# Token-mixing weights in pieces of at most 256 KB, and new instruction orders, in a two-layer attention and token-MLP kernel

## Chip, core and metric

The kernel runs on one core of a Trainium2 chip. The metric is the device time of one execution in microseconds, as the median of several runs. The core has five engines with queues of their own: TensorE (PE, with its weight loads shown as PEld), VectorE (DVE), ScalarE (ACT), GpSimd (POOL) and SyncE (SP). In this kernel SP does nothing but issue DMAs; "SPq" in a profile is SP's queue.

## What is computed

Two kinds of layer alternate, two times each, on one batch of 2048 tokens of width 512 in bf16. A is attention with 32 heads of 16 columns and a sliding window of 256 tokens; B is an MLP over the token axis (w1 is 2048 x 1792, w2 is 1792 x 2048).

```python
def _A_ref(x, wqkv, wo):
    H = 32; Dh = D // H; W = 256
    qkv = (x @ wqkv).reshape(B, S, 3, H, Dh).transpose(2, 0, 3, 1, 4)
    ...
    scores = einsum("bhqd,bhkd->bhqk", q, k) * (Dh ** -0.5)
    scores = where(mask, scores, -1e9)        # 0 <= i - j < W
    o = einsum("bhqk,bhkd->bhqd", softmax(scores), v)
    return o.transpose(0, 2, 1, 3).reshape(B, S, D) @ wo

def _B_ref(x, w1, b1, w2, b2):
    h = _layernorm(x)
    u = gelu(einsum("bsd,sf->bdf", h, w1) + b1)
    y = einsum("bdf,fs->bds", u, w2) + b2
    return y.transpose(0, 2, 1)

x = x + _A_ref(_layernorm(x), A_wqkv, A_wo)
x = x + _B_ref(_layernorm(x), B_w1, B_b1, B_w2, B_b2)
# and both once more
```

## The kernel before

Everything stays in SBUF: x as 16 tiles of 128 tokens, the normalised x (`xh_sb`), its transpose for the projections (`xhT`), masked copies of q and k, v, the probabilities (`p_sb`, seven slots) and the MLP's hidden `uT` in 14 tiles.

**Attention** runs over four groups Q of 512 tokens, four groups t of eight heads and nine steps m. A step is one `emit_scores` (matmuls on quarters of the array, L684), one exponential on ACT (`emit_exp`, L695), one or two multiplications by an edge mask (L712, on DVE or POOL), and one `emit_pv` (L733). That is 144 steps a layer. Two pairs of PSUM banks take the scores in turn, so step n + 2 waits for the exponential of step n. Between steps PE does other work: projections to q, k and v (L526), the output projection (L653), and products of the MLPs next to it. After every second head group four DMAs move denominators to `den_c` and numerators within `oU`.

**The MLP** needs all 16 token tiles for every hidden tile. `u_product` (L859) adds up one hidden tile (ft) from one quarter of the tokens, four matmuls at a time; `job_y` makes one output tile st from eight and then six hidden tiles (L932, the last tile of the kernel in two halves, L919). w1 is cut into seven blocks fb of 256 columns (two hidden tiles each), and each block into quarters q of the tokens. Blocks 0 to 2 lie in `w1buf`; they were loaded in halves of 512 KB (`w1_half_dma`). Blocks 3 to 6 borrow `xhT`, `k_sb` and `q_sb` once attention no longer needs them, in quarters of 256 KB (`w1_dma`); quarters 0 and 1 of block 3 share one tracked buffer in `xhT`, and quarters 2 and 3 the other. w2 is cut into eight blocks s2 of 256 output tokens, each loaded in two parts of 512 and 384 KB (`w2_dma`) into `w1buf` or `oU`; the later blocks follow when `job_y` has read the earlier ones.

**Order.** The program lists operations with what they read and write (`Plan.op`), and dependencies come from that. Which engine does an operation, and in what order, is written out in the tables `ORDER`: a string for each engine, in which two letters are the number of an operation in base 64 of `ALPHABET` ("AB" is operation 1, "BA" is 64). `BANKS` names the PSUM bank of each short-lived product. `emit` walks the tables and puts semaphore waits where a dependency crosses engines. An engine runs its list strictly in order; a DMA that has to wait on SP holds up all DMAs behind it. Every DMA also waits for the one that used its semaphore 16 DMAs ago.

At the start SP loads x tiles 0 and 1 (operations 0 and 1: AA, AB), tiles 2 and 3 (AC), four 256 KB parts of wqkv (AD to AG), the v part of wqkv, 512 KB into `w1buf` (AH), and x tiles 4 to 7 (AI); `turn_weights` (L437, L438) then rearranges that v part. The first normalisation (L460 to L476), a transpose on PE (L515) and its copy to `xhT` lead to half-projections (L562) and the first scores.

Of the kernel before, what the change touches and what calls it, by code (L numbers as in the profile page):

```python
# [33 lines left out]
O0OmOsO6NqPBOzO5PFM0PKPAPSQYPZPEPfPJPPPVPjPtNkPNPYPyPeP4PcPiPsQAQHPoPxP3P-QRO3QGQVQKQbP7QoQfQkRXQvQUQaQeQ1Q-Q5QjQuRDORRKQ0Q4ROQsRUQ+RHRcQERhRNRTRbRmRg
RlRzR0RRSuR3R4R5SvSrSsS3S0S4SxSGS1S2SDS6S5SRSJSySVS7SNSwStSoSlSzSpSmSqTHSnTDTFTBTZS9S8S-TaThTNTVTOTiTRTSTWTdTeTLTJT0UFT5UGT1T6UAUBUqUUUvUZUjUfUrUdUbUk
VQU8UVUhUoUwVAVEVSVIWjWkVMVWVbYeVpVkYfVhVuV1VaX5X6VyV6VjVoV+VtV0V5WGWTWoV9WNWFWVWDW4WfWaWKXYXGWRWwWrXHWZW1WeW9WqWvW0XCZoW8XBXNXUXdXrYzXiXnZeYCXwXcX1Xh
XmXvX0X-YXYMYHaNZ3YTYaX+aOYuYGYLYQY1a+Y6YZY-Yta-ZEZIYyY5Y+ZDZPalZZZHZOZSZhboZrZlZMbpZyZgZ5cLZ+ZkZqZxaCbHaKZ1aVaHZ9aiaBaJaSaeaYayadarahbEaqaaaxa6a5bDbS
cObNbldZbMbhcPbybRb2babVb6cjcDbkbtb1cIb5aucbcCcHcgdrcocNcfcsa1c0clc4eVdAcrczdEbudRc3c-dDdQdVdUdcb9ehdmdbduc7dzdfeFd5eAcvdteHdyd4d-eMgIeQeDeYeueeeLeneP
eXeberd2ezfLe7emfDejeqfIeye6fCfQe2fVfHfPfUfcfjfrfnfvgrfmfzfqfyf3gff-f2gFe+gLf+gEgQiLgYgKgPgcgVh8gkgogTgbgwgjgngvg0fYhBgzhFf6hQhkhbhAhfiohEhmhMhKhqhxhU
h0h1h4heh-hjhNhpiDhwh3iIiaiQh+iCiXiHiNiehOiiibisixiWiTidihi3iriwi2i-ili+jGjKjHjRjYkZjVjUjbjojfi6jkjajejwkAj2jjj6jskEjvj1kLjtkPj5j-kWjDkIkejEkjkOkVkdko  # L40
kiknk1k2kSkTk5k6k7lwl8l5lzl2l9l6lIltlulFl3lxlXlPl0lLlTlylvl1l4lqlrlsl7mHmJmBmPmjmDmQmFlnmTmkmblomXmfmgmUmcmYl+lpl-mLmNmzm9m+mvnDnEm5m6mwnHnIm0nNnbnjnf
# [5 lines left out]
NzMYMXMvL5MmL6MHNRM8MzMnNhL7NVNWNbMIMTN3NiNjMUMoOPOMO-N9OgN-MVOZOoPnOrOCOwOxNrM1O9QZOBPWPXPRM2PbPOPhPdP6PpPqQJO4QLQMQXP8P9QdQCQDQTRYQpQqQrQhRAQ3QyOSRB
QtP+RIRJRZRCRoRpRaRsRqRSR6R7RxQFRvSASCSHSISFSESSSKSWSXSTSOSLSPSMSQSUSYSZSbSfSgTbTPTjTTTXTfUHT7UKT2T+T3UCT-ULUDT4UEUOUMUaUTUgUeUcUsU9UlU+UmUiUnUWUxUtVC
VFUyVGUXWlUuUzUYVNU0VLVYVOU2VeVVYgYjVmVnU4ViV3VxVrX7V4WmVzWAWUWpWJV8WEW5WnWXWMW6W7X8XaWPWYYkX9WcWQXIW3XLXbZpXMYlXWXPY0XEXtXXXlXFZfXpXyYDYYX3YnYBYsYqXq
YpZ4YPYEYSYVYRY3YxaPY4Y8Y9bAZBZKZUbBanZTZNbqZuZtbCZncMZ7ZvbrZ8aAaFaIaUaXaTaZatacbJa0bGaba8aQdacQbncRbUb0aRbsbccSbWckbXcTawcGavcVcddscicqbYcucncma2cXc6  # L50
# [1016 lines left out]
```

## Time and profile before

| | us |
|---|---|
| three runs | 489.77, 489.77, 489.91 |
| median | 489.77 |
| profiled execution | 490.92 |
| its span | 489.2 |
| PE busy in the span | 480.0 (98%) |
| DVE / ACT / POOL busy | 335.3 / 319.7 / 199.6 |
| DMA moved | 43.59 MB, mean 89 GB/s |

The granted TensorE clock was 1.0. How to read it: the busy time of PE comes from pipelined matmuls whose ends are modelled, so its share is no measure of free room. An idle time stands with the engine that waited, and behind an arrow the instruction that ended the wait. A row of the table by stretches has the stretch, its length, the busy time of each engine with its number of instructions, the clock, the share of the DMA engines and the rate in GB/s. A row of the timeline has the start, the length, the engine and line, and what is written from what.

### The profile page before, as it was taken

The numbers are of one execution on the slowest core, as the hardware profiler recorded it, in microseconds if no ns is written. First come the engines' busy times: TensorE is split into PE (matmuls) and PEld (weight loads), VectorE is DVE, ScalarE is ACT, GpSimd is POOL, SyncE is SP. The second block draws the span as 40 slices with busy tenths as digits, with TensorE's granted clock in tenths as the row PEclk, the third lists the DMA queues.
The fourth block names the chain that finished last, engine by engine and source line by source line (L and its number), as shares of the span: only waits on it lengthen the run. The fifth ranks groups of instructions, "written<-read, shape, count | busy, mean of one in ns | idle before, by whom it ended". The sixth has DMA issues, their size and how long they took to land.

```text
span 489.2 us, 17263 instructions
## 1 busy us (share of the span) xinstructions
PE 480.0 (98%) x7706; PEld 255.4 (52%) x7706; DVE 335.3 (69%) x707; ACT 319.7 (65%) x391; POOL 199.6 (41%) x365
## 2 busy tenths in 40 slices
PE   7999998999999999999999999999999999999997
PEld 6544555555556444444445555556556544444444
DVE  7999998889988550246798777999977646122123
ACT  4999998999989313302767889999999940240000
POOL 5988884534726100022624544465644721000000
PEclk9999999999999999999999999999999999999999
DMA  6442024400228780350024300130222957030842
GB/s 194 92 119 56 27 60 100 70 5 27 27 58 223 215 228 1 107 147 5 1 44 132 89 27 3 37 62 6 68 70 77 261 148 204 0 98 10 228 150 86
DMA packets 83722, 43.59 MB, mean 89 GB/s; under 512 B 19008, under 2 KB 82624, under 8 KB 83648
## 3 DMA queue, kind: packets, MB, share of 16 engines
q1 hardware_dynamic: 79776, 42.48, 32.1%
q0 software_dynamic: 3872, 0.02, 1.2%
q8 instruction: 60, 0.98, 0.8%
q14 instruction: 14, 0.11, 0.1%
HBM read 32.51 MB, written 2.10 MB: 71 GB/s over the span
## 4 chain that ended last, share of the span: by engine, by line
PE 91%; ACT 5%; DMA 1%; DVE 1%; SPq 1%; issue 0%
PE ps L859 20%; PE ps L932 19%; PE ps L526 17%; PE ps L684 14%; PE ps L733 12%; PE ps L653 6%; ACT p_sb L695 4%; PE ps L777 1%; DMA x_sb<-in_A_x_dram 1%; PE ps L919 1%; SPq L352 1%; PE ps L446 0%; DVE o L358 0%; DVE q_sb L537 0%; ACT vT L360 0%
## 5 line engine op out<-in xcount | busy, mean ns | idle before, releaser
L695 ACT ACTIVATE p_sb<-ps 128x1024 bf16<-128x1024 f32 (+8 forms) x288 | 261.1, 974 | 23.5 <-PE ps L684 18.5
L712 POOL TENSOR_TENSOR p_sb<-p_sb,edge 128x256 bf16<-128x256 bf16 (+2 forms) x223 | 106.8, 494 | 102.7 <-ACT p_sb L695 88.0
L684 PE MATMUL ps<-q_sb,k_sb 64*64 64x288 bf16 (+8 forms) x2816 | 107.2, 250 | 1.4 <-ACT p_sb L695 1.1
L526 PE MATMUL ps<-xhT,wqkv 128*128 128x512 bf16 x376 | 95.6, 382 | 0.2 <-DVE q_sb L537 0.2
L733 PE MATMUL ps<-p_sb,v_all 64*64 64x288 bf16 (+8 forms) x2816 | 89.7, 246 | 1.6 <-DVE o L358 1.1
L684 PEld LDWEIGHTS ps<-q_sb,k_sb 64*64 64x64 bf16 x2816 | 53.6, 106 | 53.4 <-ACT p_sb L695 32.9
L733 PEld LDWEIGHTS ps<-p_sb,v_all 64*64 64x64 bf16 x2816 | 58.4, 107 | 14.8 <-issue 5.5
L932 PE MATMUL ps<-uT,w1buf 128*128 128x512 bf16 x280 | 64.3, 380 | 0.0
L936 DVE SCALAR_TENSOR_TENSOR x_sb<-ps,b2col,x_sb 128x512 bf16<-128x512 f32 x31 | 22.6, 745 | 51.0 <-PE ps L932 50.9
L712 DVE TENSOR_TENSOR p_sb<-p_sb,edge 128x256 bf16<-128x256 bf16 (+2 forms) x177 | 45.3, 275 | 14.1 <-ACT p_sb L695 12.7
L526 PEld LDWEIGHTS ps<-xhT,wqkv 128*128 128x128 bf16 x376 | 30.6, 98 | 39.7 <-issue 5.4
L482 POOL TENSOR_TENSOR rstd<-vare,mhalf 128x4 f32<-128x4 f32 x15 | 15.2, 1015 | 86.3 <-DVE vare L480 48.6
L859 PE MATMUL ps<-xh_sb,w1buf 128*128 128x512 bf16 x192 | 46.3, 381 | 0.0
L460 DVE BATCH_NORM_STATS2 stats<-x_sb 128x6 f32<-128x512 bf16 x64 | 42.9, 681 | 1.8 <-DMA x_sb<-in_A_x_dram 1.6
L932 PEld LDWEIGHTS ps<-uT,w1buf 128*128 128x128 bf16 x280 | 26.3, 98 | 32.3 <-issue 1.3
L537 DVE TENSOR_TENSOR k_sb<-ps,half 128x1024 bf16<-128x1024 f32 (+1 forms) x29 | 34.7, 1197 | 5.0 <-PE ps L526 4.9
L492 ACT ACTIVATE xh_sb<-x_sb,shift,rstd 128x512 bf16<-128x512 bf16 x8 | 6.4, 810 | 48.1 <-POOL shift L486 48.1
L537 DVE TENSOR_TENSOR q_sb<-ps,even 128x1024 bf16<-128x1024 f32 x29 | 35.3, 1217 | 1.9 <-PE ps L526 1.5
L932 PE MATMUL ps<-uT,oU 128*128 128x512 bf16 x154 | 35.5, 380 | 0.0
L653 PE MATMUL ps<-wo_sb,oT 128*128 128x512 bf16 x128 | 32.4, 381 | 0.0
L859 PE MATMUL ps<-xh_sb,k_sb 128*128 128x512 bf16 x128 | 30.8, 380 | 0.0
L586 POOL TENSOR_TENSOR v_all<-vB,v_all 128x512 bf16<-128x512 bf16 (+1 forms) x16 | 23.5, 1474 | 16.8 <-DVE vB L601 16.6
(89 smaller groups left out, 453.1 us busy)
## 6 DMA issues: line engine op xcount, KB each, us to landing
w1buf<-in_B_w_dram SPq DMA_DIRECT2D x20, 512.0 KB
oU<-o SPq DMA_DIRECT2D x16, 256.0 KB
k_sb<-in_B_w_dram SPq DMA_DIRECT2D x16, 256.0 KB
w1buf<-in_B_w_dram SPq DMA_DIRECT2D x10, 384.0 KB
oU<-in_B_w_dram SPq DMA_DIRECT2D x6, 512.0 KB
oU<-in_B_w_dram SPq DMA_DIRECT2D x6, 384.0 KB
q_sb<-in_B_w_dram SPq DMA_DIRECT2D x8, 256.0 KB
xhT<-in_B_w_dram SPq DMA_DIRECT2D x8, 256.0 KB
```

Source lines behind the costliest of these rows:

```text
L460: dve(lambda e: e.bn_stats(stats[:, t, :], x_sb[:, t, :]), 690, prio, reads=[R("x", t)], writes=[R("stats", t)])
L526: last = e.matmul(ps[:, b, :], lhsT=wqkv[:, c, c0:c0 + P], rhs=xhT[:, buf, c, :], start=(c == 0), stop=(c == 3))
L537: return e.tensor_tensor(dst, src.unsqueeze(2).to_broadcast([P, n, 2, w]), mask[:].unsqueeze(1).unsqueeze(3).to_broadcast([P, n, 2, w]), o ...
L586: return e.tensor_tensor(d, src.unsqueeze(2).to_broadcast([P, k, 2, DH]), v_all[:, 0:32].rearrange("p (h d) -> p h d", h=2).unsqueeze(1).t ...
L653: last = e.matmul(ps[:, b, :], lhsT=oT[:, buf, t, i * P:(i + 1) * P], rhs=wo_sb[:, t, :], start=(t == 0), stop=(t == 3))
L684: last = e.matmul(ps[64 * c:64 * c + 64, 2 * half + r, 32 * i0:32 * i1], lhsT=k_sb[rows, ring, t, kb % 16, :], rhs=q_sb[rows, t, c, 32 * i ...
L695: latest[0] = plan.op({ACT: (170 + int(2 * (512 - c0) * 0.84), lambda e: e.activation(p_sb[:, slot, :, c0:512], ps[:, 2 * half:2 * half + ...
L712: return e.tensor_tensor(v, v, g, op=ALU.mult)
L733: last = e.matmul(ps[64 * r:64 * r + 64, B_O + (c ^ r), 32 * i0:32 * i1], lhsT=v_all[rows, col:col + 64], rhs=p_sb[rows, slot, r, 32 * i0: ...
L859: r = e.matmul(ps[:, b, :], lhsT=blk[:, n, (ft % 2) * P:(ft % 2 + 1) * P], rhs=xh_sb[:, 4 * g + n, :], start=(first and g == quarters[0] a ...
L932: r = e.matmul(ps[:, b, :], lhsT=blk[:, fc, (st % 2) * P:(st % 2 + 1) * P], rhs=uT[:, fc, :], start=(fc == 0), stop=(fc == NFT - 1))
L936: dve(lambda e: e.scalar_tensor_tensor(x_sb[:, st, :], ps[:, b, :], b2col[:, st:st + 1], x_sb[:, st, :], op0=ALU.add, op1=ALU.add), 750, prio,
```

## The change

All loads of w1 and w2 are at most 256 KB. `w1_half_dma` issues two quarters, and what used to be tracked as a half of a `w1buf` block is tracked as two quarters, so that a `u_product` waits for its own quarter alone. `w2_dma` issues four parts of 4, 4, 4 and 2 hidden tiles instead of two of 8 and 6, each with its own part of the buffer; `job_y` still multiplies in steps of 8 and 6. That makes 42 more DMAs (2553 operations become 2595). All five order tables and the table of banks are new: 82 of the mask multiplications go from POOL to DVE and 86 the other way, 26 other operations from DVE to ACT and 27 back, and each engine's order differs. The operations on PE are the same.

```diff
     "tensor": """
-AuAvAwAxAyBLAzBJA0BPBNBTBRBVBXDTCuB1CeA1BpA2CjCoA3CcCyC3D1C9CnDEBtDKCxDOC2C8DXDDBxDJDeDmDNDkB5DxDVDsDbDBGsD4D9DiDrEFECDwEKFZD3D8EaEBEPGQEpEJEOETEjEeE3
+AuAvAwAxAyBJAzBLA0BPBNBTBRBVBXDTA1CeB1BpCoA2CjCuC3CyCcD1A3DEC9CnBtCxDKC2C8DODkDXDeDDDJDNDVDbDmBxDsDxDBB5D9DiD4DrGuDwECEKEFFaEPD3EaD8GSEjEBEJEOETEqEeEv
 ...
     "scalar": """
-AjAlBMBQBUBWBYDUB2CfBqCkCpAoCzC4C+DFBuDLDPDYByDfDnDlDtDyDCD5D+EDELEGEbEQEqEkEUE4EvEfE9FCEzFKFPFWFdFTFyF5F+GDGJGNGUGeGmGqIDGwG3G+HDHHHPHWHfHjHsHzH7IAIJ
+AlAjAiBMBQBUBSBYAmAnCfB2CpCkCvC4CzD2C+DFBuDLDPDYDfDnByDdDyDtB6D+D5GvEDELEGEQEbEkErEwEfE5E+E0FDFLFQFXFeFUFzF6F-GEGLGPGWGgGoGsGyG5HAHFHJHRHZHiHmHvH2H+ID
 ...
     "sync": """
-AAABACADAGAEAIAHCiAFCwDjCsDIDSCtC7DWDqHKGgGhEXEWG6EYEZGaGbGZGcKlEnK+IYIaKkIbHRLOIZKTKfKdKeKgMZMcMbMaOcObOaOdP2TxQPQNQQPwPrQOOWIvQiQzQnRfTnRyR8R+R9OlRk
-R-SkLkSiQ9GGRGTzTySjTlTmToTwT9UIT8UJWCVfVgWSXJYhXRXQXKXSXTYiZ2ZdZcaGZVZXZWZYbebdbfbgdpeUdqeEdkdjdidlfffidxfhfghTgDhZhYhXhamrhijPjNiqjQi1mnjOmsivj+j0e5
+ABAAACAIAEADAGAHAFCiCwCsDjCtDSDIC7G8GiEWHMEZDWEXEYGjEnEoDqGdGcGbGeIcIbLTIdHTHUIeKqLDKpKjKiKkKlMfMhMgMiKXKYOhOiOgOjQTQUQtQoQVQWP2P8RDPxR4OcRlQ5SDSCSERM
+SFSqRqSpIyIzSoT6T7T8T9OrGHGILpLqT+T-UAUBTrTsTtTuTvTwTxTyUYUZUaUbUKULUMUNWkVyVxWUY1Y2Y3Y4XbXcXdXeXmXkXnXlaMZzZyacZrZtZsZubzb2b0b1eAebd-erd5d6d4d7f4f3fQ
 ...
-        load(w_nat, w_src[:, :, 2 * D:3 * D], 1 << 19, -100, writes=[R("w1", 2, 0)])
+        load(w_nat, w_src[:, :, 2 * D:3 * D], 1 << 19, -100, writes=[R("w1", 2, 0), R("w1", 2, 1)])
 ...
-                return w1buf[:, fb, 4 * q:4 * q + 4, :], [R("w1", fb, q // 2)]
+                return w1buf[:, fb, 4 * q:4 * q + 4, :], [R("w1", fb, q)]
 ...
         def w1_half_dma(fb, h, prio):
-            load(w1buf[:, fb, 8 * h:8 * h + 8, :], w1v[:, 8 * h:8 * h + 8, fb * 256:(fb + 1) * 256], 1 << 19, prio, after=latest,
-                 writes=[R("w1", fb, h)])
+            for q in (2 * h, 2 * h + 1):
+                load(w1buf[:, fb, 4 * q:4 * q + 4, :], w1v[:, 4 * q:4 * q + 4, fb * 256:(fb + 1) * 256], 1 << 18, prio, after=latest,
+                     writes=[R("w1", fb, q)])
 ...
-                return flat[:, 0:NFT * 256].rearrange("p (f s) -> p f s", f=NFT), [[R("w1", k, h)] for h in range(2)]
+                return flat[:, 0:NFT * 256].rearrange("p (f s) -> p f s", f=NFT), [[R("w1", k, h)] for h in range(4)]
 ...
-                    [[r for t in (2 * h, 2 * h + 1) for r in held_o(k - 2, t)] for h in range(2)])
+                    [held_o(k - 2, t) for t in range(4)])
 ...
-            for h, (lo, hi) in enumerate(W2_PARTS):
+            for h, (lo, hi) in enumerate(((0, 4), (4, 8), (8, 12), (12, NFT))):
                 load(dst[:, lo:hi, :], w2v[:, lo:hi, s2 * 256:(s2 + 1) * 256], (hi - lo) << 16, prio, reads=after, writes=held[h])
 ...
-                pe(f, 217 * (hi - lo), prio, reads=held[part] + [R("uT", fc) for fc in range(lo, hi)], writes=[BK(b)])
+                pe(f, 217 * (hi - lo), prio, reads=held[2 * part] + held[2 * part + 1] + [R("uT", fc) for fc in range(lo, hi)], writes=[BK(b)])
```

More of the change, by code (lines that the diff above doesn't have):

```diff
@@ L34 @@
[L34 to L41, printed above, removed]
@@ L47 @@
[L47 to L50, printed above, removed]
@@ new lines @@
+NYLsLWL0LaNRL7LlMDLiLrMILzL6MQMCL3MVMHMPMjNHMrMnMUMcMvN2MzMmM3L+M-MqMyNENmNKM2M+NTNWNdNDNjMYNtNJNQNaNzNgN7NiN-OUNsOMNyN6OQPEOZN+OLOkOPOWOdOoOtOvOnOsOz
+PsO6OyPANwO5PHO-PLQeM6PYPGPKPQPPPbPlPVPfPTPzPePkPpPoNqP+P4PiPyQGP3P9PuQNQFQMQXO9QQQbQhRdQuQlQqOXQaQ1QgQkQpQ7RFQ-Q0RJQBRQQ6Q+RERUQKRaRNRiRXRnRTRZRhRmRs
+RrR5R6QyS0R9R+R-S3S6S7S9SxS1TASMS+S4SJTBS2SXSPSySTSbS8S5SrSsS-TCStTLTTTNTUSzTHTjTJTXTDTfTbSuTcTYTkTgTnToSvSwTFTPTRUCUDUHUQURUIUVUWVBU8U9U1UxUvU2UrUtVC
+U6UzUmVOViVaVkVzVSUnW1VoVtW2VWV7V2YyWEYzWAWHVsV1VeYNWMV6WQV-WGWLWYW6YOWPWnWfWlWVWXWxWcWsXKXsXYWjXCW9Z+XZXHWrWwXPW8ZJXUXoXBZ0XxXGXOXTXhX2YWX-X7YEXwX1Yr
@@ new lines @@
+YJYTX6ajYbYDYIYgaNYnYSYaYfYuakZEYkZLbUZQYtZDZIZVZPZaa7ZeZUZZZlbVZdZvZkZoZ3b+Z7aBZib-aIaPZ2chZ6aUaAaHaYbdaLagaradaTa4aXafaoa0aubIazbBa3baawbAbQbHbPbZbo
+ckbjb7biclbnb3bwcMdvcIb6cDcZc5cQbrcLcecPbEcxcYcdc2eBc+cjdCbLc1dKc7dOesdWdBdJdacEdndNdVdrcTdydZdmd8e4eEdqeKdFeQdxd1eXeceeeDeJePejdReneWeaevfFe1eie+gheN
+emfCfKeueyfjfTe9fbe6fgfBfJfSfofNftfafffnfsf0f7f-gDhEgHgLg4f+gPgCgKgXfWgegOgWgkilgpgdgxiWg1gjgogug9gshBhJfwhNg0g8hAhah+hehIhMhZhqhdhmhuh1gSjCh5iAhkiEiO
+iLh4h9iSiPiZiDiKidhniiiRiYiqi0ixicihini4i1i8jGhojLiwi3i7jRitjFjZjKjQjYjhi-jrjgjkjvjyj1kzjuj5j0j+kakCkKj4j9kQjUkUkJkPkTkekZkiklkGkskpkwkHktk4k9jdkolCkv
@@ new lines @@
+k3k8lBlQlPjelTlUlVmQmWmHmNmKmRmIlimSmJlfmXmTlpllmLmUlxmVltmMmOmPmEmFmGmYmfmdmtmum1mxmhmjmpmymbm5mqm6m2m9mBmCm+mDmZmnmlnVnpnhndntnqnunenWninRnSn5n1oJn6
+oFoBn2oVoGoNoCoKoWoRoZoSoOoaogod""",
+    "vector": """
+AcAdAeAfAgAWAUAVAaAYA7A5A8AQA6BBA-A9BDBAA+BFBEBKBIBHBdBOARBfAXBWBZBbAhDUBgAbAZBqBrBcCgBaBeBhBsBjCrChCdFjBoC0BnC1FlAsBmDGFhBvDlBwFnFiDcDgFoBzDoDCFmFkDu
+DzFpFrB0JJB7EAB8D0JNFbEHGTEUEVEsENJKEIEgEhE1E-ExGlFAF4JPFVFMFYFNJLFGFHF1HpFIGBHqGQGGHrHcJMIGGaGZHOIHGzIIG+G0JOJQG1HGJTIUHLHWHXHeIVHjHnHfI5JRH3H-HzHyIA
@@ new lines @@
+INIXIOKsIoIaIZItIpIlKaI6JuJFJbH5JBJVJcIqI8JHJ6JlJkH6JiJ7K2KEKAKFJvLwH7J8JwKGKVLhKIKgLVLxKLMMKNKMLILFK7K8LRLZLfNZLcLbNSLjLkMFL9MKL4L5MTLyNIMeMdMsN3MXN4
+MxL-MAMNM1NnM5NGN5NoNXNpMZNcNbNhMOMtNlOVMBMuOCODPFOTObOeOfOuOFOmOqOxMaPtNxPCO2O1QfO3M7POPaPcPWPXPnPdPUP1PjP7M8PvPwM9O+QRQIQJQdReQPQvQSRfOYQ4RGQ9QnRHQw
+QCRPROQDQxRYQERgRIRwRuRpQzRyR8SBSASGQLSISNSOR3SKSLSYSQSZSUSRScSdSeSVSSSaSWShSfSkSmTVTdTlThTpTZUEUJUOUSUFUXUcUTUGUPUUUdUgUeUjUlUyUwUsUuU+U3U4VDU0U-VjU5
+VAV0VcUoVQUpVRUqVTVEW3VFVvVUVwVIVGVXVMVNVVVnVYY0VZV+VfVKVqY5V4V5WJVgW7WOYPWmWpYQYRWhVhWiWdXMWeXNW4WbW5XuY6XaW0XfZKXRZ1XXXvXiXgXqY7YAXrYBY9ZBYsYLX+YHYV
@@ new lines @@
+YdYeYiaOYmYpZGYlalZHYxZOYYZSZTZca8YZama9bWa-a+ZpZjcAZ5aEbXaFciaSaaabaGaDaWaeaiaqapavbfanbKa6bDaxaybSbqbccBcCbYcmbybxbhdwcOc6cnbtbGbucobFcpeCc0c4bMcrc8
+c9cwcvcFetcUdtducVcGd+e5d3d2dGeddSeTfGdHeUeheZfHdIeqeOe0ezfkdTe8e7fdflfVfPdUfOf2bNgEfrf1cHhFhGg5gFgGg6bOfXdggNfYimdefZiXg7hHgvgwhRgtgzdldjfxhLg-hQhch-
+hThYfyhXhvhsjDhhhliHiCh3iQfziNiJikgUifizipi2ioigi+hpiviujTjOjAjbjmjBjtjljcjxk0j7kDkMkbkNjVkEkck1kdkWkFk2gVjWjXlGkXkIlIkrkylElFk-lSlNkulWjflclMleljlklh
+lglqlrlmlnlslylzlulvlol0lwl3l1l7l6l5mvmzmrm3m7m-nXnjnrnTnvnfn7n3oHoXoDoLoToPobohoe""",
+    "scalar": """
@@ new lines @@
+AlAjAiBMBQBUBSBYAmAnCfB2CpCkCvC4CzD2C+DFBuDLDPDYDfDnByDdDyDtB6D+D5GvEDELEGEQEbEkErEwEfE5E+E0FDFLFQFXFeFUFzF6F-GEGLGPGWGgGoGsGyG5HAHFHJHRHZHiHmHvH2H+ID
+IMIRIgIkA4IsIwI2I-JEJaJfJnJrJzJ3J-KDKQKUKdKnKvKhKzK5LALHLMLQLYLeLnNPLtL1L8MEMJMRMWMkMoMwM0M4NANFNLNUNeNkNuN0N8OAONOROaOlOpOwO0O7PBPIPMPZPRPmPgP0PqNrP5
+P-QHQOQYQcQiQmQrQ2Q8RARKRRRVRbRjRoRtR7R2SHR1SlTMTKTITETOTWTeTqTiTaTmTGSnTQTSU7VPVbVlVpVuV8V3WFWIVLWBWNWZWRWoWgWWXLWyWtXtXDW+Z-XIXQXVXpXyX3XjX8YFYXYKYC
+YUYcYhYoYvZFZMZRZWZbZfZmZwZqZ4Z8aCaJaQaVaZbeasaha5a1bJbCbbbRbpbgbkb8b4cNcJcacRbscfcyc3c-dDdLdPdXdbdodsdzd9eFeLeReYefekeoewe2e-gifDfLfUfcfhfpfuf8gAgIgM
@@ new lines @@
+gQgYgfglgqgyg2g+hChKhOhbhfhrhwh2gTh6T5iBiFiMiTiIiaieijiriyi5i9jHjMjSjajijsjwj2jzj6j-kLkRkVkfkmkjkkkqkxk5k+lDlRlXl9lKldmemgmimwmkm4msm0mcm8manAmomm""",
+    "gpsimd": """
+AJAMAKANASALATAOAPBCBGCEB+CJCDCHCKAoCLArCCCBCMCNApCOB3CqClAqBiB4BkCmBlC5AtC-DHDADMC6CPAkDZDaCQDhDQDRDpCRFqFsD-DvFtFvCSEED6D7FwCTERCUEMElEcESEmFuEdEtCV
+CWE6EyE7FEE2FRFZFfFSF0FgGACXCYF7GFF8GXB9GMGhGRCZHsGtGpHBG6B-HCHKG2HSHaIJCIHwJSJUJWIEISIWJYIhCAJXIxCGJACFI3JgJoJsJ0J4I7KRKeKoKHKJKwKWK6K0KKLBLNLJLSK9L2
+LoLuMGMSMpCaMlNBNCNfNVNMNNN1NvOBN9OOOSOEOGOIOKOHPDO8PJOJPNO4PSPhMbPrP6CbQAQZQjQsQ3RBRCRLRWRSRcRkRvRxRzR0SgSiSjUfUhTzUiUkVmT1T4T3VdV9VHVJVrWCWDWKT2WSWa
@@ L66 @@
+WzWTWqWuXEW-XAXJXFWvT0XWXSX4XzY8X0YGY+ZCX5ZAX9Y-YMYjYwZNYqZXZYZgZnZhZxZ9aKaRata2bTblbmb9b5cKcbcccgcSczbvcqcsdAcudEdQdMdYdcctdpddd0cWeGcXeMeSegexeVepel
+fIfEfAe3fMfifefqgBfvf9gJfmgZgggagmgRgrdfgng3dhdihShDdkhPhghUhWhVh7iUiGibiVi6isjIjNjjj3kAkSlHkglJknlLk6l2l4l8""",
     "sync": """
[L67 to L68 removed]
@@ L70 @@
+nUnsoEoMnooQoUocoIoiof""",
 }
 BANKS = (
-    "76766776777676767667766666677676777767776666667677677767666776666776676767677677667767766777666767676776776666677766676776776676677676676676"
-    "766677666777777667666776777676766767776666776776766776677766")
+    "76676666677777767667766677767676676777766766677677667767776667766766677776777667676766677676677766767676766667676766676776776676676677676676"
+    "766667776776766777666667676776766767776677777666676767677677")
 class Res:
@@ L438, in turn_weights @@
                      ACT: (360, lambda e: e.activation(d, o, ACTF.Copy))},
-                    reads=[R("w1", 2, 0)], writes=[R("wqkv", 2, t, r)], prio=-96)
+                    reads=[R("w1", 2, 0), R("w1", 2, 1)], writes=[R("wqkv", 2, t, r)], prio=-96)
         for t in range(4):
@@ L921, in f @@
                         return r
-                    pe(f, 1530, prio, reads=held[0] + held[1] + [R("uT", fc) for fc in range(NFT)], writes=[BK(bank)])
+                    pe(f, 1530, prio, reads=sum(held, []) + [R("uT", fc) for fc in range(NFT)], writes=[BK(bank)])
                     dve(lambda e, half=half, bank=bank: e.scalar_tensor_tensor(
```

23 lines of the change are left out of this document (3 added, 20 removed).

## The prediction

> **What bounds the kernel now.** I read the page's busy shares first, then cut the span at the first and last exponential of each attention (an ACT answer of the timeline gives 14.62, 159.38, 235.30 and 393.76 us) and asked for a table of these five stretches, then for ACT's own waits inside them.
>
> ```profile
> PE 480.0 (98%) x7706; PEld 255.4 (52%) x7706; DVE 335.3 (69%) x707; ACT 319.7 (65%) x391; POOL 199.6 (41%) x365
> ```
>
> ```profile
> core 0: us, PE busy (x) PEld busy (x) DVE busy (x) ACT busy (x) POOL busy (x), PEclk, DMA share, GB/s
> 0.00:14.62 14.62, 11.25 (x127) 9.15 (x128) 11.29 (x41) 7.90 (x14) 9.32 (x28) 1.00 0.54 163
> 14.62:159.38 144.76, 141.91 (x3272) 80.45 (x3269) 132.02 (x272) 138.52 (x165) 94.43 (x177) 1.00 0.34 74
> 159.38:235.30 75.92, 75.92 (x460) 35.02 (x459) 33.66 (x66) 20.36 (x31) 9.76 (x12) 1.00 0.40 112
> 235.30:393.76 158.46, 158.14 (x3332) 87.37 (x3330) 130.49 (x282) 140.33 (x167) 82.12 (x144) 1.00 0.27 71
> 393.76:489.20 95.44, 92.77 (x526) 43.41 (x523) 27.83 (x48) 12.62 (x20) 3.97 (x7) 1.00 0.40 113
> ```
>
> The rows say: the two MLP stretches (75.9 and 95.4 us) are PE and nothing else. The first attention is ACT's: 138.5 of 144.8 us busy, 6.2 us idle. The second attention is shared: ACT is idle for 18.1 us of 158.5, DVE for 28.0, and PE shows 158.1 us busy, which the page warns is not PE at its peak. Who keeps ACT waiting stands in its waits, of the first attention and of the second:
>
> ```profile
> ACT p_sb L695 <- PE ps L684: 4.9, 12, 1.4
> ```
> ```profile
> ACT p_sb L695 <- PE ps L684: 13.6, 27, 1.1
> ```
>
> So in the second attention ACT waits 13.6 us for scores that PE delivers late, because y and projection work is threaded between them; there the order on PE matters. No line of PE's own waits names a DMA. A weight that comes late would be a new wait.
>
> **How I read the diff.** Two letters of a table are an operation's number, so both sets of tables can be written out and compared entry by entry; a split load takes two numbers. SP's list grows from 194 to 236 entries (10 halves of w1 and 32 halves of w2 become pairs). In all 42 places the two pieces follow each other directly, so no other transfer is slipped between them. What is new comes from the order of whole loads, from readers that wait for one quarter, and from the moved instructions.
>
> **Start.** Three lines hold the first exponential back:
>
> ```profile
> 10.25 0.69 DVE L460 BATCH_NORM_STATS2 stats<-x_sb 128x6 f32<-128x512 bf16 x1 [0.91 <-DMA x_sb<-in_A_x_dram]
> 11.32 0.77 PEld L562 LDWEIGHTS ps<-xhT,wqkv 128*128 128x128 bf16 x8 [0.93 <-DVE xhT L358]
> 14.62 1.92 ACT L695 ACTIVATE p_sb<-ps 128x1024 bf16<-128x1024 f32 x2
> ```
>
> DVE stands 0.91 us for x tiles 4 to 7, the copy of xhT queues behind it, and PE's second half-projection waits for that copy. In the new table this x load is SP's fourth entry, not its seventh (AI follows AC), ahead of three 256 KB weights, so it no longer holds DVE. Against that, DVE now builds five edge tiles before its first statistics, about 0.3 us late, and ACT runs two weight turns (0.42 us each) before its first exponential. Followed through with the rows' durations: first statistics 3.1 (was 2.87), half-projections at 9.9 and 10.9 (were 9.64 and 11.32), three masks of 0.84 us on ACT end at 13.0, the turns at 13.85. That is 0.8 us sooner than 14.62; without the turns' cost elsewhere it could be 1.5, with a late weight 0. Taken: **-0.8** (-1.5 to 0).
>
> **First attention.** ACT's extras between its 144 exponentials change by: one v copy less (0.61), one k mask less (two of 0.64), two o copies less (1.20), one turn (0.42) and one reciprocal copy (0.31) less; two q masks more (2.54) and one u copy more (0.62). Sum **-0.6**, on the engine that sets the end. DVE gains some 1.2 us of work here beside 12.7 us idle; I price it at nothing, and at +1.2 if that cover is gone. Masks of p change hands between DVE and POOL (82 one way, 86 the other), which leaves the sum of each nearly alone.
>
> **First MLP: the rush of loads.** After the last score SP issues the rest of w1. Before:
>
> ```profile
> 167.19 0.77 SPq L352 DMA_DIRECT2D k_sb<-in_B_w_dram  x1
> 168.00 0.62 SPq L352 DMA_DIRECT2D xhT<-in_B_w_dram  x1
> 168.66 0.66 SPq L352 DMA_DIRECT2D w1buf<-in_B_w_dram  x1
> 173.40 0.37 SPq L352 DMA_DIRECT2D xhT<-in_B_w_dram  x1
> ```
> ```profile
> 158.50:178.00 19.50, 19.50 (x174) 9.08 (x173) 11.83 (x24) 4.20 (x6) 1.62 (x3) 1.00 0.80 223
> ```
> ```profile
> 178.60 1.89 PE L859 MATMUL ps<-xh_sb,xhT 128*128 128x512 bf16 x8
> ```
>
> SP stood 4.0 us before 173.40 for the landing of the piece issued at 168.00, which shares xhT's buffer; so a 256 KB piece took 5.4 us in this crowd. The new order keeps those two far apart, and SP's stand goes. But it puts w1's fb 3, quarter 1 after three den_c loads and twelve more, among them four w2 pieces (896 KB) whose reader comes some 59 us later. PE first needs that quarter one u step of 0.86 us sooner than at 178.60, about 177.7. Twelve issues at 0.62 us after 163.73 give an issue at 171.2. Bytes from 158.5 on: 1.05 MB of w1 released by the last scores, then 3.28 MB up to and with this quarter, 4.33 MB. At the best rate that the slices show (261 GB/s at a share of 0.95, so 275 at most) it lands near 176; at the 223 GB/s of the row above, near 179.5. Price 0 to +3.4 (the start moves the need 0.8 sooner); I take **+0.5**, nearer the fast end, since the old rush had SP's 4.0 us stand in it, which lowers its rate. The Trainium skill ("DMA: Bandwidth & Descriptors", section "Anatomy of one DMA") gives a transfer about 2.0 us and its bytes over 436 GB/s: by that an estimate for 256 KB is 2.6 us where the row has 5.4, the rush would take 10 us, and this term would be 0; the trace speaks against the rate under load.
>
> **Second attention.** Six y matmuls (1.3 us at the 0.216 us that 120 take in 25.90 us of the chain) and two projections (1.7 us) move from the first MLP behind the second attention's first score. The MLP loses 3.0 us; the attention gains 3.0 if PE is its limit, nothing if PE only waits there. They land in its first 20 us, where ACT is busy for 60 to 80% of a slice and PE is the limit, so most comes back. In the rest the filler is spread more evenly: counted in full-size matmuls between scores, 18 steps at a time, it ran 38, 42, 36, 32, 40 after the first 36 steps, and now 40, 42, 36, 36, 36. ACT gets 3.0 us of extras more, beside 18.1 us idle. Bounds -3.0 to +1.5; taken **-1.0**, from the even spread and a third of the moved work.
>
> **Second MLP and end.** 16 w2 loads become 32 pieces; the tightest, for y tile 9, is released 7.8 us of PE work before its use (7.4 before). The issues cost SP 42 x 0.37 to 0.77 us = 16 to 32 us over the span, on a queue that mostly waits. The output stores come in another order, the last half tile last as before. Priced at **0** (0 to +1.5).
>
> **Sum.** -0.8 - 0.6 + 0.5 - 1.0 + 0 = -1.9 us. The profiled execution took 490.92 us with a span of 489.2 (1.7 us lies around it) and is 1.15 over the median of 489.77, so the median becomes **487.9**, a profiled span 487.3. A measurement of this kernel can tell about 0.2%, 1.0 us, from no change.
>
> **Rivals.** (a) *A late weight on PE.* Place: the first u step on fb 3 in the first MLP, with a twin in the second, where fb 5's quarter 2 is read 6.5 us of PE work after the last PV and issued 2.6 us after it. It decides if the first lands after 177 us. At 223 GB/s PE stands 2.5 to 3.4 us; a 5.4 us flight makes the twin 1.5 us late. With the other gains: 489.77 - 2.4 + 3.0 + 1.5 = 491.9, slower. For: SP's list, with w2 ahead of w1. Against: no PE wait on a DMA in the old trace with a similar crowd. 0.29. (b) *Nothing.* The pairs stay together, so splitting does nothing but double issues; the start's gain is eaten by the first attention, where 6.2 us of ACT's idle time moves about. 489.5; 0.15. (c) *Larger gain.* Half of the 13.6 us that ACT waits for scores in the second attention goes, 5 us after DVE's part: 485.0; 0.11.
>
> **How the numbers follow.** Forecast 0.45 at 487.9 (own range 486.3 to 489.0, its top just over the 1.0 us line), (c) 0.11, (b) 0.15, (a) 0.29. Faster takes the forecast and (c), less a little: 0.55; within 0.2% takes (b): 0.15; slower 0.30. The range reaches from (c) to (a): 485.0 to 492.0; a lateness of both stages beyond 3.4 and 1.5 us, or a gain over 5, is left out.
>
> **What would show it.** First exponential near 13.9 us. First attention 143.5 to 145 us long, with ACT's idle time near 6. No gap of SP like that before 173.40. PE's waits: a line "<- DMA xhT<-in_B_w_dram" would mean (a). The second attention with ACT waiting less than 13.6 us for L684; more than that would make the forecast wrong there, as would a first exponential after 14.6.

## The result: 0.17% slower

The changed kernel took 490.66 us (median of 13 runs, 489.1 to 491.43) against 489.67 us for the kernel before (13 runs, 488.82 to 490.15): ratio 1.0017, 95% interval 1.0009 to 1.0025. The forecast of 487.9 us was 2.8 us too low, and the sign was wrong.

The profiled execution after took 490.62 us, close to its median; its span is 488.9 us. That of before, 490.92 us, was 1.25 us over its median, so the two profiles laid side by side (488.9 against 489.2) hide the loss. The five stretches of the changed kernel, cut as before at the first and the last exponential of each attention:

```profile
core 0: us, PE busy (x) PEld busy (x) DVE busy (x) ACT busy (x) POOL busy (x), PEclk, DMA share, GB/s
0.00:13.29 13.29, 11.64 (x132) 10.38 (x132) 10.41 (x36) 8.52 (x15) 7.79 (x24) 1.00 0.65 199
13.29:158.15 144.86, 142.29 (x3271) 80.00 (x3264) 133.54 (x278) 138.39 (x162) 98.56 (x181) 1.00 0.28 61
158.15:230.71 72.56, 71.81 (x440) 33.10 (x439) 31.31 (x62) 15.99 (x25) 7.25 (x11) 1.00 0.51 139
230.71:393.90 163.19, 162.39 (x3353) 89.62 (x3350) 133.51 (x291) 144.42 (x172) 78.08 (x141) 1.00 0.23 62
393.90:488.90 95.00, 92.19 (x523) 43.36 (x522) 29.60 (x52) 11.82 (x20) 2.11 (x3) 1.00 0.43 125
```

The start is 1.33 us shorter, the first attention as long as before, the first MLP shorter and the second attention longer. The prediction's table cut before's first MLP at 235.30 us; by the start of the next exponential in the trace it ends at 234.27, so before's stretches are 14.62, 144.76, 74.89, 159.48 and 95.44 us. All stretches below are cut at the exponentials in this way. The two rows of before that change by it:

```profile
159.38:234.27 74.89, 74.89 (x455) 34.53 (x454) 32.90 (x65) 19.34 (x29) 8.73 (x12) 1.00 0.40 113
234.27:393.75 159.48, 159.16 (x3337) 87.86 (x3335) 131.24 (x284) 141.34 (x168) 83.14 (x144) 1.00 0.27 71
```

ACT's waits for scores, in the first and then in the second attention, hardly moved in sum (4.9 and 13.6 us before):

```profile
ACT p_sb L696 <- PE ps L685: 5.2, 12, 0.9
```
```profile
ACT p_sb L696 <- PE ps L685: 14.4, 22, 2.8
```

What is new stands in PE's waits (engine, line, what it waited for; total, times, longest, in us). Before, none of them named a DMA:

```profile
PE ps L527 <- DMA xhT<-xh_sb: 0.9, 1, 0.9
PE ps L861 <- DMA xhT<-in_B_w_dram: 0.8, 1, 0.8
```

(A third, 0.2 us for a part of wqkv, lies in the start.) The second is the quarter of w1 that the prediction priced. SP's timeline and PE's show its issue, behind the four w2 pieces, and its reader:

```profile
167.79 3.97 SPq L353 DMA_DIRECT2D oU<-in_B_w_dram  x4
171.81 0.61 SPq L353 DMA_DIRECT2D xhT<-in_B_w_dram  x1
```
```profile
177.21 1.89 PE L861 MATMUL ps<-xh_sb,xhT 128*128 128x512 bf16 x8 [0.76 <-DMA xhT<-in_B_w_dram]
```

Issued at 171.81, it releases PE at 177.21: 5.4 us, the flight that before's row had. The Trainium skill's figure ("DMA: Bandwidth & Descriptors", section "Anatomy of one DMA"), by which the prediction's estimate was 2.6 us, is a fit to single transfers on GpSimd's path. This one was issued by SP, in a rush of loads, so the 5.4 us do not test the figure, and it is no price for this wait. The first wait, for a transpose of xhT near 46 us, was in no step of the prediction.

### The profile page after: what moved, and what is told of

Same layout as the page of the kernel before. It is cut to its first block, busy times and chain, and to the rows that moved or that the text cites. A ratio compares the mean times of both kernels' runs of the same rounds, so it can differ in the third digit from the quotient of the medians.

```text
span 488.9 us, 17313 instructions
## 1 busy us (share of the span) xinstructions
PE 480.3 (98%) x7706; PEld 256.5 (52%) x7706; DVE 338.4 (69%) x716; ACT 319.1 (65%) x391; POOL 193.8 (40%) x358
## 4 chain that ended last, share of the span: by engine, by line
PE 81%; ACT 6%; DMA 4%; POOL 3%; SPq 2%; DVE 1%; issue 1%; POOLq 0%
PE ps L934 19%; PE ps L861 17%; PE ps L527 14%; PE ps L685 13%; PE ps L734 10%; ACT p_sb L696 5%; PE ps L654 5%; SPq L353 2%; POOL p_sb L713 2%; DMA wqkv<-in_A_wqkv_dram 1%; POOL xh_sb L490 1%; DMA xhT<-in_B_w_dram 1%; PE ps L778 1%; DMA xhT<-xh_sb 1%; DMA x_sb<-in_A_x_dram 1%
## 5 line engine op out<-in xcount | busy, mean ns | idle before, releaser
L696 ACT ACTIVATE p_sb<-ps 128x1024 bf16<-128x1024 f32 (+7 forms) x288 | 261.4, 974 | 23.4 <-PE ps L685 19.6
L713 POOL TENSOR_TENSOR p_sb<-p_sb,edge 128x256 bf16<-128x256 bf16 (+2 forms) x227 | 110.5, 500 | 127.8 <-ACT p_sb L696 108.9
L713 DVE TENSOR_TENSOR p_sb<-p_sb,edge 128x128 bf16<-128x128 bf16 (+2 forms) x173 | 45.1, 279 | 15.2 <-ACT p_sb L696 11.6
L538 DVE TENSOR_TENSOR k_sb<-ps,half 128x1024 bf16<-128x1024 f32 (+1 forms) x28 | 33.4, 1194 | 5.5 <-PE ps L527 5.3
L538 DVE TENSOR_TENSOR q_sb<-ps,even 128x1024 bf16<-128x1024 f32 x26 | 31.7, 1218 | 2.9 <-PE ps L527 2.7
L909 ACT ACTIVATE uT<-ps,b1col 128x512 bf16<-128x512 f32 x16 | 10.4, 680 | 31.1 <-PE ps L861 31.1
L861 PE MATMUL ps<-xh_sb,k_sb 128*128 128x512 bf16 x128 | 30.6, 379 | 0.0
L906 DVE TENSOR_TENSOR v_all<-v_all,ps 128x512 f32<-128x512 f32 x12 | 8.1, 687 | 29.4 <-PE ps L861 29.4
```

The lines of the kernel that those rows point to most:

```text
L538: return e.tensor_tensor(dst, src.unsqueeze(2).to_broadcast([P, n, 2, w]), mask[:].unsqueeze(1).unsqueeze(3).to_broadcast([P, n, 2, w]), o ...
L696: latest[0] = plan.op({ACT: (170 + int(2 * (512 - c0) * 0.84), lambda e: e.activation(p_sb[:, slot, :, c0:512], ps[:, 2 * half:2 * half + ...
L713: return e.tensor_tensor(v, v, g, op=ALU.mult)
L861: r = e.matmul(ps[:, b, :], lhsT=blk[:, n, (ft % 2) * P:(ft % 2 + 1) * P], rhs=xh_sb[:, 4 * g + n, :], start=(first and g == quarters[0] a ...
```

## The experiments

All kernels keep the reference's whole computation. "The tables" are the orders of the five engines and the bank assignment. Four kernels ran on each of three chips; each ratio is to the kernel before on the same chip.

**Which half of the change.** Four kernels: before once more; before's tables with the loads in pieces; the new tables with the loads whole; and the new tables up to the first exponential only, before's from there, in pieces.

> The kernel before, unchanged, once more, for its stage lengths in another execution. The profiled execution of before took 490.92 us, 1.25 over its median. Theory 'untypical profile': the stages of this run sum to a span near 487.9, and the missing 1.2 us shows in one or two named stages (first attention 143.5 to 144.3 instead of 144.76, or second MLP under 95). Theory 'filler': the stages agree within 0.3 us each with the first profile and the rest is spread. The ratio to before should be 1.000 within 0.001 in either case.

> The order tables of before, with every load of w1 and w2 split into its pieces at the place where the whole load stood. Theory 'filler': splitting costs nothing, ratio 1.000 (0.999 to 1.001). Rival 'split': the 42 extra issues on SP cost about what the whole change costs, ratio 1.0015 to 1.003, with PE or SP waits on DMAs that before did not have.

> The new tables with the pairs of pieces put together again, each as one load at the place of the pair. Theory 'filler': the same time as the changed kernel, ratio 1.0012 to 1.0025. Rival 'split': the time of before or better, ratio 0.996 to 1.000.

> The new orders for everything that the changed kernel started in its first 13.2 us (the start up to the first exponential), the old orders for the rest, with split loads. Theory 'filler': the first exponential at 13.3 to 13.6 us instead of 14.62 and the gain kept to the end of the first attention, so 488.4 to 488.9, ratio 0.9975 to 0.998. Theory 'absorbed': the first exponential is early but the first attention grows by as much, ratio 0.9995 to 1.0005.

```diff
 e2, e4: w1_half_dma, w2_dma in pieces as in the changed kernel
-e2: the new ORDER and BANKS       +e2: before's, a split load's two numbers in its place
-e4: the new ORDER and BANKS       +e4: new for what started before 13.2 us, then before's
-e3: pieces                        +e3: whole loads; each pair of the new ORDER is one entry
```

Measured: before again 491.66 us, ratio 1.0013 (0.9995 to 1.0032); pieces alone 490.22, 0.9985 (0.9971 to 1.0000); tables alone 491.16, 1.0002 (0.9987 to 1.0016); new start alone 491.12, 0.9998 (0.9984 to 1.0012). The times settle little: on this chip the kernel before, at 491.07 us, itself ranged over 4 us (488.93 to 492.96). e1 fits neither of its theories: its profile is long again (span 490.7 us), with a first attention 1.1 us longer than in the first profile. e2 rules out "split" and lies a little below the band of "filler". e3 lies between its two bands, and e4's time is that of "absorbed". The traces settle more. The table gives, in us, when some exponentials start (numbered from 0), where the first attention ends, and what all that follows it takes (first MLP + second attention + second MLP); later runs, all but e8, are in it too.

| kernel | no. 0 | 30 | 36 | 66 | 72 | first attention ends | the rest |
|---|---|---|---|---|---|---|---|
| before | 14.62 | 44.11 | 48.49 | 77.58 | 85.82 | 159.38 | 74.89 + 159.48 + 95.44 = 329.81 |
| e1 before again | 14.63 | 44.45 | 48.84 | 77.93 | 86.91 | 160.47 | 330.21 |
| e2 pieces alone | 14.07 | 43.41 | 47.80 | 76.89 | 84.41 | 157.97 | 330.00 |
| e3 tables alone | 13.11 | 44.11 | 50.17 | 78.88 | 85.16 | 159.06 | 72.93 + 163.23 + 94.86 = 331.02 |
| e4 new start alone | 12.49 | 44.46 | 48.82 | 78.23 | 85.67 | 159.19 | 329.95 |
| after | 13.29 | 44.22 | 49.52 | 78.22 | 84.25 | 158.15 | 72.56 + 163.19 + 94.99 = 330.74 |
| e5 transposes first | 12.25 | 43.26 | 49.55 | 78.35 | 84.37 | 158.28 | 330.93 |
| e6 weight first | 12.59 | 43.56 | 49.76 | 78.47 | 84.50 | 158.40 | 71.65 + 163.20 + 95.00 = 329.85 |
| e7 den_c first | 13.79 | 43.63 | 48.02 | 77.12 | 83.96 | 157.34 | 329.84 |
| e9 after again | 12.22 | 43.20 | 49.25 | 77.96 | 83.98 | 157.88 | 73.02 + 163.19 + 94.99 = 331.20 |
| e10 both first | 12.22 | 43.09 | 47.62 | 76.33 | 82.56 | 156.46 | 71.65 + 163.19 + 95.00 = 329.84 |
| e11 pieces, den_c first | 14.66 | 45.27 | 49.66 | 78.75 | 87.34 | 160.72 | 329.94 |
| e12 filler back | 12.93 | 44.33 | 50.05 | 78.76 | 84.78 | 158.68 | 74.67 + 159.47 + 95.59 = 329.73 |

Three things follow. What comes after the first attention depends on the tables to within some tenths of a microsecond; the differences between runs of one kernel arise in the start and the first attention (and, in the changed kernel, in how late its weight is in the first MLP). With before's tables they arise above all between exponentials 66 and 72, which take 8.24, 8.98 and 7.52 us in before, e1 and e2, and 6.03 us in after. And a start that is 2.1 us sooner (e4) is gone by exponential 30. In e4 a part of that is the hybrid's own, since PE stands 1.06 us at 13.50 us, where the two orders meet. But the changed kernel shows the same without a seam: its first exponential is 1.33 us sooner than before's, its exponential 30 is 0.1 us later.

**Four single edits.**

> The changed kernel, with SP's list altered in one place: the last two DMA transposes of the third query block's xhT are issued ahead of the den_c and wo loads instead of behind them. In the changed kernel's trace PE stood 0.9 us (and its weight load 1.1 us) for xhT before a projection of that block, near 48 us. Theory 'late transpose': the start's gain of 1.3 us is lost there, so this kernel is 0.9 us faster than the changed kernel (0.2% below it, about equal to the kernel before), and the line PE ps L527 <- DMA xhT<-xh_sb is gone. Rival 'absorbed': ACT, not PE, sets the pace of the first attention, so its first exponential's gain is used up by ACT's own work anyway; the wait may go, the time stays that of the changed kernel (1.002 of before).

> The changed kernel, with w1's fb 3, quarter 1 issued ahead of the four w2 pieces that stand in front of it on SP. In the changed kernel's trace PE stood 0.76 us for that quarter at 177.2 us. Theory 'late weight': the wait is in a stretch where PE is the limit, so the first MLP is 0.7 to 0.8 us shorter (72.56 to about 71.8 us) and the kernel is as much faster than the changed one. Rival 'absorbed': the second attention's first stretch gives it back, first MLP plus second attention stay 235.8 us.

> The kernel before, with one entry of SP's list altered: the den_c load that stood behind a transpose and a 512 KB piece of w1 (issued at 79.3 us) is issued together with the other two den_c loads, ahead of them. Theory 'late den_c': the copy of o that waits for it held PE and ACT near 82 us for 0.4 to 1.8 us, differently in every run; without that wait the six exponentials from number 66 take near 6.1 us (8.24 in the profile of before), the first attention is 143 us or shorter, the kernel is 0.8 to 2 us faster than before, and its runs spread less. Rival 'absorbed': the time lost there would have been lost at a later place of the first attention anyhow; within 0.1% of before, spread as before.

> All loads in pieces as in the changed kernel; orders of the changed kernel for everything that started before the end of its first attention (157.5 us), and the order of before for all that follows. Theory 'moved filler': first MLP plus second attention take 234.4 us as with the old orders and not 235.8, the second MLP 95.5 and not 95.0; the kernel is 0.9 us faster than the changed one, so 0.999 to 1.0 of before. Rival 'chip and run spread': the loss is not in the second attention's order but scattered, so the kernel is as slow as the changed one, 1.002.

```diff
 SP's list, e5 (after's, 34 to 46 us):
-xhT, xhT, den_c, xhT, oU, wo, den_c, den_c, xhT, w1, w1, wo
+xhT, xhT, xhT, xhT, den_c, oU, wo, den_c, den_c, w1, w1, wo
 SP's list, e6 (after's, 167 to 172 us):
-w2, w2, w2, w2, w1 fb 3 q 1
+w1 fb 3 q 1, w2, w2, w2, w2
 SP's list, e7 (before's, 73 to 80 us):
-den_c, den_c, xhT, oU, w1 (512 KB), xhT, den_c
+den_c, den_c, den_c, xhT, oU, w1 (512 KB), xhT
 e8: after's tables to 157.5 us, then before's; pieces
```

The kernel before took 490.53 us on this chip.

*e5*: 492.58 us, ratio 1.0041 (1.0022 to 1.0060). A miss: the wait for xhT went and another took its place. DVE's and PE's timelines, of the run of 490.94 us:

```profile
46.16 0.69 DVE L358 COPY o<-ps 128x512 f32<-128x512 f32 x1 [2.22 <-DMA den_c<-o]
```
```profile
47.26 0.41 PE L733 MATMUL ps<-p_sb,v_all 64*64 64x288 bf16 x8 [1.51 <-DVE p_sb L712]
```

With the transposes first, the den_c loads, which read the buffer o, were issued at 43.55 us, not 40.90; DVE's next copy into o stood 2.22 us for them, the masks behind it came late, and PE stood for those. Exponential 36 starts at 49.55, as in after. So neither "late transpose" nor "absorbed" was right as put: the limit is SP's queue, where transposes and den_c loads compete, with wo in front of some of them. (The profile is of the lowest of its twelve times; what makes the median 1.6 us longer is not in it.)

*e6*: 489.89 us, 0.9974 (0.9959 to 0.9989). PE's wait at L860 for a DMA is gone, the first MLP is 71.65 us (72.56 in after) and the second attention unchanged, by its windows:

```profile
158.40:230.04 71.64, 71.22 (x432) 33.20 (x439) 31.32 (x62) 15.99 (x24) 7.27 (x11) 1.00 0.51 141
230.04:393.24 163.20, 156.34 (x3312) 89.64 (x3350) 133.51 (x291) 144.43 (x172) 78.24 (x141) 1.00 0.23 62
```

"Late weight" holds: 0.9 us, and with it all of the excess of what follows the first attention is gone (329.85 us against 329.81 in before).

*e7*: 489.11 us, 0.9966 (0.9948 to 0.9985), its runs within 1.4 us of each other (488.58 to 489.95) where before's spread over 4.8. SP's timeline of before, then DVE's copy in before again and in e7:

```profile
77.20 0.58 SPq L352 DMA_DIRECT2D w1buf<-in_B_w_dram  x1
77.84 1.39 SPq L507 DMA_TRANSPOSE xhT<-xh_sb  x1
79.28 0.69 SPq L352 DMA_DIRECT2D den_c<-o  x1
```
```profile
83.27 0.69 DVE L357 COPY o<-ps 128x512 f32<-128x512 f32 x1 [2.30 <-issue]
```
```profile
80.07 0.69 DVE L357 COPY o<-ps 128x512 f32<-128x512 f32 x1
```

In before, a small den_c load stands behind a 512 KB weight and a transpose; the copy into o waits for it, 2.30 us in this run. (The profile names no releaser there; that it is this load is shown by the edit.) In e7 the copy does not wait, and exponentials 66 to 72 take 6.84 us; near 6.1 was expected, and a first attention of 143 us or less, which takes 143.55. The gain lies within the 0.8 to 2 us that "late den_c" gave. The kernel before thus had a wait of its own that the new tables lack: 1.1 and 1.8 us on PE in its two profiles, 0.4 us with the loads in pieces.

*e8*: 494.32 us, 1.0080 (1.0050 to 1.0110). A miss, and of the hybrid's own making: where the two orders meet, a weight in q_sb is late. The second attention and second MLP are as expected (159.49 and 95.59), but the first MLP takes 81.18 us. PE's timeline and its windows (the last three columns: granted clock, DMA share, GB/s):

```profile
166.39 1.04 PE L860 MATMUL ps<-xh_sb,q_sb 128*128 128x512 bf16 x4 [2.25 <-DMA q_sb<-in_B_w_dram]
```
```profile
164.00:166.00 2.00, 0.15 (x1) 0.00 (x0) 0.00 (x0) 0.00 (x0) 0.00 (x0) 1.00 1.16 299
166.00:168.00 2.00, 1.61 (x7) 0.72 (x8) 0.00 (x0) 0.00 (x0) 0.00 (x0) 0.93 1.03 255
168.00:174.00 6.00, 4.20 (x40) 1.87 (x40) 2.53 (x4) 1.01 (x2) 0.00 (x0) 0.50 1.03 298
174.00:176.00 2.00, 2.00 (x39) 0.83 (x38) 0.59 (x1) 0.00 (x0) 0.00 (x0) 0.86 1.17 310
```

PE stands 2.25 us, and soon after it resumes its granted clock is 0.50 for some 7 us, so the stretch loses more than the wait. The question of this kernel was left to e12.

**Both waits, and the moved work.**

> The changed kernel as it is, beside the other three and before on one chip. Theory 'late weight': 1.7 us of its loss stand in two waits of PE for DMAs (0.9 us near 46 us for xhT, 0.76 us at 177 us for w1's fb 3, quarter 1), so it is 0.7 to 0.8 us slower than a kernel without the second of them. Rival 'run spread': its ratio to before moves with the chip, since before's own runs range over 4 us; then 0.999 to 1.002, with a profile like the first one.

> The changed kernel with two edits of SP's list: w1's fb 3, quarter 1 ahead of the four w2 pieces, and near 40 us the order transpose, oU, transpose, two den_c loads, then wo and w1, so that neither the transpose nor the den_c loads stand behind a 256 KB weight. Theory 'SP's order': both waits go, exponential 36 starts near 48.3 us instead of 49.5, and the time is 1.4 to 2.0 us under the changed kernel's, 488.6 to 489.3 where that has 490.7. Rival 'one wait for another': as when all transposes were put first, den_c comes late instead and DVE's copy of o stands; then exponential 36 stays near 49.5 and only the 0.8 us of the weight are gained.

> The tables of before with the loads in pieces, and the den_c load put ahead of the 512 KB piece's two halves as in the run of before with that load first. Theory: with that wait gone, pieces are worth nothing by themselves (0.1 us); same time as the run of before with den_c first, 0.9966 of before. Rival 'pieces help': smaller pieces shorten other waits behind large loads too; 0.5 us or more below it, 0.9955 or less.

> The changed kernel with w1's fb 3, quarter 1 issued first, and from 229 us on (before the second attention's first exponential) the order of before: the six y matmuls and two projections that the new tables moved behind the second attention's first score are back in the first MLP. Theory 'conserved': PE is the limit on both sides, moved work costs the same in either place: first MLP about 74.1 us, second attention about 159.5, second MLP 95.5, sum 329.1 to 329.9, the same total as with the weight first alone (329.85). Rival 'filler costs': the moved work delays ACT in the second attention, so putting it back gains 0.5 to 1.0 us (sum 328.9 to 329.3).

```diff
 e9: none
 e10: e6's edit, and SP's list at 34 to 46 us:
-xhT, xhT, den_c, xhT, oU, wo, den_c, den_c, xhT, w1, w1, wo
+xhT, xhT, den_c, xhT, oU, xhT, den_c, den_c, wo, w1, w1, wo
 e11: before's tables with e7's edit, loads in pieces
 e12: e6's edit; after's tables to 229 us, then before's
```

The kernel before took 490.32 us on this chip. *e9*, the changed kernel: 491.19 us, 1.0007 (0.9987 to 1.0026), so its distance to before does move with the chip and before's spread, and on this chip it is not told from zero. PE's waits for DMAs:

```profile
PE ps L526 <- DMA xhT<-xh_sb: 1.7, 1, 1.7
PE ps L860 <- DMA xhT<-in_B_w_dram: 1.2, 1, 1.2
```

Its first exponential came 1.07 us sooner than in the first profile of the changed kernel, and the wait for xhT was 0.8 us longer: that wait is where a start that is earlier still is given back.

*e10*: 488.43 us, 0.9958 (0.9941 to 0.9975), 2.76 us under e9, and no run of the one within the range of the other (487.81 to 489.12; 490.15 to 491.91). PE's wait for xhT and SP's timeline in after, then SP's in e10:

```profile
46.38 1.04 PE L527 MATMUL ps<-xhT,wqkv 128*128 128x512 bf16 x4 [0.91 <-DMA xhT<-xh_sb]
```
```profile
40.27 0.58 SPq L353 DMA_DIRECT2D wo_sb<-in_A_wo_dram  x1
40.90 1.40 SPq L353 DMA_DIRECT2D den_c<-o  x2
42.34 1.22 SPq L508 DMA_TRANSPOSE xhT<-xh_sb  x1
```
```profile
38.90 0.62 SPq L352 DMA_DIRECT2D oU<-o  x1
39.57 1.29 SPq L507 DMA_TRANSPOSE xhT<-xh_sb  x1
40.90 1.40 SPq L352 DMA_DIRECT2D den_c<-o  x2
42.34 0.41 SPq L352 DMA_DIRECT2D wo_sb<-in_A_wo_dram  x1
```

The last transpose is issued at 39.57 us (42.34 in after) and den_c still at 40.90, because wo now comes behind both. Both waits are gone, exponential 36 starts at 47.62, the first attention ends 1.42 us sooner than in e9 and the first MLP is 1.37 us shorter. "SP's order" holds, and this kernel is faster than both. The gain is above the 1.4 to 2.0 us expected, since both waits are longer in e9 (1.7 and 1.2 us) than in the profile from which it was worked out (0.9 and 0.8).

*e11*: 489.34 us, 0.9980 (0.9961 to 0.9999). No gain over whole loads with den_c first (489.11 us, on another chip). Its profile is of a run of 492.41 us (the other eleven: 488.80 to 490.33), where DVE's copy did not wait but PE stood 1.9 us at 86.1 us, before a projection from xhT. A late transpose is likely there: the one issued at 79.65 us, behind the two pieces of w1, has its last semaphore update in the trace at 85.84 us, just before PE's weight load at 85.90. No run tests it. In e7 that transpose was issued at 77.32 us.

*e12*: 489.95 us, 0.9981 (0.9962 to 1.0000). Its windows for the three stretches after the first attention:

```profile
158.68:233.35 74.67, 74.09 (x445) 34.57 (x453) 33.02 (x66) 17.86 (x28) 10.44 (x14) 1.00 0.48 135
233.35:392.83 159.48, 153.44 (x3298) 87.85 (x3335) 131.23 (x284) 141.35 (x168) 82.79 (x143) 1.00 0.26 71
392.83:488.40 95.57, 92.25 (x516) 43.49 (x523) 27.62 (x48) 12.63 (x20) 4.05 (x7) 1.00 0.40 113
```

Their sum, 329.73 us, is that of e6 and e10 (329.85, 329.84), with 3 us of PE's work on the other side of the border. "Conserved" holds, to 0.1 us.

## Why the prediction was wrong

**Start (-0.8).** Right in kind, too small: -1.33 us in the first profile, -1.7 to -2.4 in e5, e6, e9, e10 and e12, whose lists are alike there. But it was carried into the sum as if it reached the end, and it does not.

**First attention (-0.6).** This step failed. It took the stretch to shorten by what ACT's extras lose. They did lose 0.6 us (11.7 to 11.1 us by the rows of the two profiles), but ACT's busy time fell by only 0.13 us (138.52 to 138.39) and the stretch not at all (144.76 to 144.86). The runs show three things in its place. The first is where the extras stand: up to exponential 30 every kernel with the new tables takes 30.9 to 31.4 us, and before, e1, e2 and e7 take 29.3 to 29.8 (e11 30.6). Before and after, by their windows:

```profile
14.62:44.11 29.49, 29.34 (x499) 15.19 (x496) 28.68 (x66) 28.66 (x44) 25.85 (x58) 1.00 0.50 111
13.29:44.22 30.93, 30.00 (x497) 15.20 (x490) 30.20 (x68) 29.61 (x44) 27.97 (x62) 1.00 0.38 88
```

Of these 1.4 us, 0.95 are ACT's own work (28.66 to 29.61), which it saves only later; the rest is idle time of ACT. That uses up the start's gain. No single edit tests it, so why the new order costs there stays open. The second is SP's queue, which the step did not look at; the lists were compared, but only the rush of the first MLP was priced. In the new list a transpose of xhT stands behind wo and two den_c loads. Between exponentials 30 and 36 after loses 0.9 us on before (5.30 us against 4.38); e10's edit of SP's list there brings 4.53, where e9, with the same start, takes 6.05. The third is a gain: the new tables lack before's late den_c load (6.03 us from 66 to 72, against 8.24 in the profile). Set against a typical run of before, whose first attention would end near 158.1 us if its profile's 1.25 us of excess lies there, as the table's spread suggests, the changed kernel's 158.15 is no gain: start and first attention together brought 0 where -1.4 was predicted.

**First MLP (+0.5).** Right in place and mechanism; 0.76 us in the first profile, 1.2 in e9. The quarter was issued at 171.81 (171.2 was worked out) and released PE at 177.2; PE asked for it 1.2 us sooner than the 177.7 put there (177.21 less 0.76). That the landing lies between the two given (176 and 179.5) is in part luck. The sum does not come to them: 4.33 MB from 158.5 us on take to 174.2 us at 275 GB/s and to 177.9 at 223. And the queue was at the fast rate:

```profile
158.50:177.20 18.70, 17.95 (x165) 8.35 (x165) 11.31 (x22) 1.83 (x3) 1.34 (x3) 1.00 0.99 266
```

At 266 GB/s that is 5.0 MB by the landing, more than the sum counted. This is rival (a), without its twin: no PE wait names a DMA in the second MLP. Its price of 2.5 to 3.4 us was too high here; e8 shows that a wait of that size would have cost more still, through the clock.

**Second attention (-1.0) and second MLP (0).** The second step that failed. The prediction let a third of the moved work be hidden and the even spread gain something. Nothing was hidden: first MLP -2.33, second attention +3.71, second MLP -0.45, together +0.93 us, of which 0.76 is the late weight. ACT's 13.6 us of waiting was taken as room; it grew to 14.4 while ACT's busy time there went from 141.34 to 144.42 us. In that stretch PE is the limit by its own work, and ACT's idle time is only its shadow: e12 moves the work back, and the sum of the three stretches stays.

**Sum.** Start and first attention 0 (by the estimate above), the late weight +0.76, the rest +0.17: +0.9 us, against 0.99 by the medians. The loads in pieces had no effect of their own that these runs could tell from before's spread, as rival (b) had it, which also had the start's gain eaten by the first attention; what cost, by the stretches, was the tables.

## What to carry to other kernels

A term that makes one stretch start earlier is worth only what the stretch behind it lets through: before adding it to a sum, look at what the limiting engine has to do there first, and walk the next in-order queue's list to the next reader, small transfers and transposes included, and see what large load stands in front of each. Where two stretches in a row both have PE as their limit, work moved across the border is worth zero, whatever idle time another engine shows there. And when one kernel's runs spread more than another's, find the stretch that varies between two profiles of the same kernel: here it led to one small transfer behind a large one, and moving that alone took 1.42 us off the kernel before.
